# Zero matmuls in every early gap of TensorE, and the first q and k of two head pairs transposed as one planned step

## The chip, the cores and the metric

The kernel runs on one core of a Trainium2 chip. The metric is the device time of one execution in microseconds (us). A profile shows one execution: its span runs from the first to the last instruction, and its own device time stands a little above the span. Engines are written as the profile writes them: PE is TensorE (PEld its weight loads), DVE is VectorE, ACT is ScalarE, POOL is GpSimd and SP is SyncE.

## The reference

Attention over a sliding window of 128 positions with 4 sink positions, for 4 batches, 8 heads, 768 positions and a head dimension of 64, followed by a feed-forward part over all 3072 tokens:

```python
scores = scale * np.matmul(q, k.transpose(0, 1, 3, 2))
keep = is_sink | in_window                  # rel in [0, 128), or position < 4
a = softmax(np.where(keep, scores, -1e9))
x = np.matmul(a, v).transpose(0, 2, 1, 3).reshape(B * S, H * D)
a, b = x @ w1, x @ w2                       # 512 -> 1024
out = (a * b @ w3) @ w_out                  # 1024 -> 1024 -> 512
```

## The kernel before

The whole kernel is a list of steps (class `Op`, L126) that a planner puts in order while the program is built. Each step names its engine, a planned duration, the steps that it depends on, the buffers that it takes and frees, and a priority. The loop at L843 simulates five engines: it takes whatever step can start first, calls the step's function, which writes its instructions to the engine's queue, and books the planned time. The chip then runs each engine's queue in exactly that order, held only by semaphores. So a planned time that changes a little early can reorder steps much later, and a planned time has no power over the chip beyond the order.

Work on TensorE falls into these groups. Batch 0's q and k are transposed (L441) from two layouts in `early` (`early_72` is k and `early_71` is q), copied from PSUM to `qkT` (the copy helper, L143), and multiplied to scores (L597). ScalarE takes the exponential (L615), VectorE multiplies by a mask (L621), TensorE multiplies by v (L673), and VectorE normalises (L683, L688) into `xs`, which is transposed again (L709). The product w3 · w_out is computed once ("the fold"): w3 is transposed in pieces (L351 for the first three row blocks, by column block j; L382 for the other five row blocks) and multiplied by w_out (L359 and L389). The feed-forward part is L753 (x · w1 and x · w2), L768 (their product, on VectorE) and L783 (times the fold), and the result is stored by SP (L800). For batches 2 and 3, q and k are transposed by DMA on SP's queue (L487), and `xs` by L729.

The start is this. ScalarE and SP issue four fast loads of the first two head pairs of k and q (L215; here called k0, q0 for the pair r = 0, and k1, q1 for r = 1), with planned landings of 3.75, 4.05, 5.2 and 5.5 us (L887). k0 and k1 are cast by VectorE and q0 and q1 by ScalarE (L235). All other loads are issued by POOL (L160), one after another in the fixed order of `LOADS` (L243), and at most eight of them are in flight at a time. POOL also builds `ident`, `pick` and `tri` between its loads.

The transposes of a head pair are six matmuls for k and six for q, into one PSUM bank. If (c, r) is in `APART` (L173), the planner has two steps, `a` for k and `a2` for q (L451, L452); otherwise one step that depends on both casts (L454). Their results are copied by two steps, `tk` (k's half) and then `tq` (q's half), each on ScalarE or VectorE, whichever the planner finds free (L457, L458).

Before TensorE starts a step, the planner looks at the gap since its last one (L854). If the gap is over 0.12 us and the plan stands before 45 us, it puts in matmuls of a tile of zeros (L862) into a free PSUM bank, as many as fit the gap less 0.05 us, at most 24 at a time. A matmul over 128 columns is planned at 0.056 us, and at twice that while the plan stands before `WARM` = 5.8 us (L805, L855). These zero matmuls are ordinary instructions: once in the queue they run whether or not real work is waiting behind them.

Of the kernel before, what the change touches and what calls it, by code (L numbers as in the profile page):

```python
# [21 lines left out]
def kernel(  # L22
# [22 lines left out]
    P = 128  # L45
# [92 lines left out]
    PE, ACT, DVE, POOL, SP = "pe", "act", "dve", "pool", "sp"  # L138
# [6 lines left out]
    def cols(n, k=1):  # L145
        return k * (n / 2400.0 + 0.0025)
# [23 lines left out]
    DEEP = 2  # L170
    FUSED = (1, 2, 3)
    KINDS = (0, 2, 2, 2)
    APART = ((0, 0), (0, 1))  # L173
    QK_BY_DMA = ((2, 0), (2, 1), (3, 0), (3, 1))
    X_BY_DMA = ((2, 0), (2, 1), (3, 0), (3, 1))

# [102 lines left out]
    for key in LOADS.split():  # L279
        n = [int(x) for x in key[2 if key[:2] == "wo" else 3 if key[:3] == "w3j" else 1:].split("-") if x.isdigit()]  # L280
# [52 lines left out]
    acc_keys, n = [], 0  # L333
# [85 lines left out]
    for b in range(B):  # L419
# [10 lines left out]
        if b == 0:  # L430
            for c in range(NC):
                for r in range(NP):
# [16 lines left out]
                    pr = base + 1 + r * 0.1  # L449
                    if (c, r) in APART:  # L450
                        a = Op(PE, cols(P, 3) + 0.12, lambda f=tps: f((0,)), [got["k", b, c, r], op_ident], pr, takes=["mm"])  # L451
# [352 lines left out]
    free = {PE: 1.0, ACT: 0.8, DVE: 0.9, POOL: 0.9, SP: 0.8}  # L804
    WARM = 5.8  # L805
# [9 lines left out]
    def unsure(at):  # L815
        return 0.0 if at < 40.0 else 0.5 if at < 56.0 else 2.5
# [11 lines left out]
    def best(e):  # L828
        pick_ = None
        for o in ready[e]:  # L830
            w = wants(o, e) if e != POOL or o is in_order[0] else None
            if w is None:
                continue
            at = max(w, free[e])
            wait = at - free[e]
            key = (0.0 if wait < 0.05 else wait, o.prio, o.serial)
            if pick_ is None or key < pick_[0]:
                pick_ = (key, at, o)
        return None if pick_ is None else (pick_[1], pick_[2])

    with tc.manual_schedule():
        left, lanes = len(ops), []
        while left:  # L843
            moves = []
            for e in free:
                got_ = best(e)
                if got_:
                    moves.append((got_[0], e, got_[1]))
            start, e, o = min(moves, key=lambda x: (x[0], x[1]))
            if e == POOL and hasattr(o, "dma"):  # L850
                if len(lanes) >= 8 and lanes[-8] > start:
                    free[POOL] = lanes[-8]
                    continue
            if e == PE and start < 45.0 and start - free[PE] > 0.12:  # L854
                one = cols(P) * (2 if free[PE] < WARM else 1)  # L855
                n = min(24, int((start - free[PE] - 0.05) / one))
                bank = next((rings[x].slots[i] for x in ("mm", "sc", "av") for i, f in enumerate(rings[x].free)
                             if f is not None and f <= free[PE]), None)
                if bank is not None and n > 0:
                    view = bank[:, 0, 0:P] if len(bank.shape) > 2 else bank[:, 0:P]  # L860
                    for i in range(n):
                        nc.tensor.matmul(view, zeros[:], zeros[:], start=True, stop=True)  # L862
                    free[PE] += n * one
                    continue
            o.slot = {}
            for i, n in enumerate(o.takes):
                f, s = rings[n].soonest()
                rings[n].free[s] = None
                key = (n, i) if o.takes.count(n) > 1 else n
                o.slot[key] = rings[n].slots[s]  # L870
                o.slot["#", key] = s
            turn_of[0] = o.ran = e
            o.fn()
            us = o.us_on[e] * (2 if e == PE and start < WARM else 1)
            free[e] = start + us
            o.done = start + us + o.lat
            if hasattr(o, "turn"):
                dma["at"] = max(dma["at"], start + 0.6) + o.turn
                o.done = max(start + 2.2, dma["at"] + 0.9, dma["sp"] + o.pitch)
                if o in op_vst:  # L880
                    o.done = max(o.done, 11.0)
                else:
                    dma["sp"] = o.done
                    if start < 120.0:
                        o.done += LATE
            if o in st:
                o.done = (3.75, 4.05, 5.2, 5.5)[st.index(o)]  # L887
            if hasattr(o, "dma") and e == POOL:
                dma["at"] = max(dma["at"], start + us + 0.1) + o.dma * 1.02
                while dma["fetch"] and dma["at"] > dma["fetch"][0][0]:  # L890
                    dma["at"] += dma["fetch"].pop(0)[1]
                lanes.append(dma["at"] + LAND)
                o.done = lanes[-1] + unsure(dma["at"])
            for h, n in o.frees:
                h = h[0] if isinstance(h, list) else h
                key = n
                ring = n[0] if isinstance(n, tuple) else n
                rings[ring].free[h.slot["#", key]] = o.done
            for e_ in o.us_on:
                ready[e_].remove(o)  # L900
            if e == POOL:
                in_order.pop(0)
            for u in o.users:
                u.missing -= 1
                if not u.missing:
                    for e_ in u.us_on:
                        ready[e_].append(u)
            left -= 1
# [35 lines left out]
```

## Time and profile before

| what | value |
|---|---|
| runs | 199.4, 200.13, 199.81, 199.07 us; median 199.6 us |
| the profiled execution | 199.4 us, its span 197.7 us |
| TensorE matmuls busy | 191.2 us, 97% of the span |
| VectorE busy | 115.3 us, 58% |
| ScalarE busy | 98.3 us, 50% |
| POOL busy | 73.2 us, 37% |
| zero matmuls (L862) | 79, the first at 1.3 us, the last at 21.3 us |
| transposes of batch 0's q and k (L441) | 96, from 4.6 to 37.0 us |

How to read it: the chain of waits follows the work that ended last back to the start, so each piece on it held the next. A timeline line gives the start, the time to the end of the last instruction in the group, the engine, the line of code, the tiles, the count, and in brackets how long the engine was idle before and who released it. A matmul's time in the trace holds its latency, so the spacing of a group is its time less that of one matmul, divided by the count less one. The 1.7 us between span and time is the same start and end around any execution.

### The profile page before, as it was taken

What the parts mean: (1) busy time and instruction counts of PE and PEld (TensorE: products, weight loads), DVE (VectorE), ACT (ScalarE), POOL (GpSimd) and SP (SyncE); (2) the same over time, 40 slices, a digit from 0 to 9 for tenths busy, and PEclk for the clock granted to TensorE, in tenths of its full rate; (3) what the DMA queues carried; (4) which work ended last, traced back from release to release, by engine and by line L of the source; (5) the groups of instructions that cost most, each with busy time, mean ns of one, the idle gap of its engine ahead of it and who ended that gap; (6) DMA issues with size and microseconds to landing.
All of it is one profiled execution on the core that took longest, in us unless ns stands there. A gap on an engine that the chain in (4) does not pass through costs nothing.

```text
span 197.7 us, 4514 instructions
## 1 busy us (share of the span) xinstructions
PE 191.2 (97%) x1815; PEld 116.8 (59%) x1815; DVE 115.3 (58%) x262; ACT 98.3 (50%) x158; POOL 73.2 (37%) x96
## 2 busy tenths in 40 slices
PE   7989999999999999999999999999999999999993
PEld 6665655546665665567566555655665555555442
DVE  3886523668579756887877763446887543424200
ACT  3785432765466248537547623335477424243233
POOL 7997454787997385656740000000000000000000
PEclk9999999999999999999999999999999999999999
DMA  6999999999999999999999626645503434010133
GB/s 169 175 177 190 202 202 195 182 175 162 153 143 180 148 149 141 210 158 155 155 129 173 86 84 169 149 83 109 133 2 84 107 121 121 0 53 0 56 127 138
DMA packets 98181, 26.42 MB, mean 134 GB/s; under 512 B 86896, under 2 KB 94576, under 8 KB 98160
## 3 DMA queue, kind: packets, MB, share of 16 engines
q0 software_dynamic: 73584, 14.29, 91.6%
q1 hardware_dynamic: 23888, 11.38, 26.9%
q10 hardware_dynamic: 688, 0.46, 0.7%
q8 instruction: 14, 0.23, 0.5%
q14 instruction: 7, 0.06, 0.1%
HBM read 29.39 MB, written 6.29 MB: 181 GB/s over the span
## 4 chain that ended last, share of the span: by engine, by line
PE 87%; DMA 5%; POOL 4%; ACT 1%; DVE 1%; issue 0%
PE mm L753 42%; PE mm L783 21%; PE av L673 7%; PE sc L597 5%; DMA big<-in_moe_w_dram 5%; PE mm L389 5%; POOL big L160 3%; PE mm L862 2%; PE mm L470 1%; ACT qkT L143 1%; PE mm L709 1%; PE mm L382 1%; PE mm L535 1%; PE mm L441 1%; DVE qkT L143 1%
## 5 line engine op out<-in xcount | busy, mean ns | idle before, releaser
L753 PE MATMUL mm<-xT,w_sb 128*128 128x384 bf16 x512 | 89.5, 326 | 0.0
L753 PEld LDWEIGHTS <-w_sb 128*128 128x128 bf16 x512 | 48.1, 98 | 32.1 <-issue 1.4
L768 DVE TENSOR_TENSOR ab<-a_sb,mm 128x384 bf16<-128x384 f32 x64 | 35.4, 553 | 31.4 <-PE mm L753 29.8
L615 ACT ACTIVATE ex<-sc 128x1024 bf16<-128x1024 f32 (+2 forms) x49 | 44.0, 938 | 7.9 <-PE sc L597 6.6
L783 PE MATMUL mm<-w3o,ab 128*128 128x512 bf16 (+2 forms) x208 | 45.9, 363 | 0.0
L143 ACT COPY a_sb<-mm 128x384 f32<-128x384 f32 x51 | 24.4, 479 | 41.1 <-PE mm L753 22.0
L621 DVE TENSOR_TENSOR am<-ex,maskt 128x1024 bf16<-128x1024 bf16 (+2 forms) x49 | 29.8, 624 | 0.9 <-ACT ex L615 0.8
L783 PEld LDWEIGHTS <-ab 128*128 128x128 bf16 x208 | 18.6, 98 | 17.7 <-issue 0.6
L160 POOL DMA_DIRECT2D vN<-in_v_dram x24 | 21.2, 884 | 11.2 <-DMA near<-in_q_dram 3.2
L143 ACT COPY o_sb<-mm 128x512 f32<-128x512 f32 (+2 forms) x21 | 11.5, 546 | 24.2 <-PE mm L783 24.1
L673 PEld LDWEIGHTS <-am 128*128 128x128 bf16 x352 | 17.1, 97 | 3.5 <-DVE am L621 0.2
L673 PE MATMUL av<-vN,am 128*128 128x65 bf16 x352 | 19.0, 194 | 0.0
L688 DVE TENSOR_TENSOR xs<-av,rec 128x384 bf16<-128x384 f32 x32 | 17.7, 555 | 0.6
L597 PE MATMUL sc<-qkT 64*128 64x128 bf16 (+1 forms) x248 | 14.7, 241 | 0.2 <-ACT ex L615 0.2
L683 DVE RECIPROCAL rec<-av 128x6 f32<-128x6 f32 x32 | 6.2, 194 | 14.1 <-PE av L673 14.0
L160 POOL DMA_DIRECT2D big<-in_q_dram x12 | 10.6, 886 | 6.3 <-DMA vN<-in_v_dram 3.0
L673 PE MATMUL av<-vsb,es 128*128 128x130 bf16 x64 | 12.9, 220 | 0.0
L160 POOL DMA_DIRECT2D big<-in_k_dram x12 | 10.5, 880 | 3.2 <-DMA vN<-in_v_dram 1.7
L597 PEld LDWEIGHTS <-qkT 64*128 64x128 bf16 x248 | 8.1, 94 | 5.6 <-issue 4.0
L143 DVE COPY qkT<-mm 128x384 bf16<-128x384 bf16 (+1 forms) x13 | 6.8, 554 | 5.8 <-PE mm L470 3.1
L389 PE MATMUL mm<-big,w3t 128*128 128x512 bf16 x40 | 9.5, 380 | 0.1
L143 DVE COPY w3t<-mm 128x1024 bf16<-128x1024 bf16 (+1 forms) x8 | 4.5, 564 | 6.8 <-PE mm L382 6.0
(63 smaller groups left out, 142.5 us busy)
## 6 DMA issues: line engine op xcount, KB each, us to landing
out_dram<-o_sb SPq DMA_DIRECT2D x23, 256.0 KB
vN<-in_v_dram POOLq DMA_DIRECT2D x24, 128.0 KB, 9.7
w_sb<-in_moe_w_dram POOLq DMA_DIRECT2D x8, 256.0 KB, 10.3
big<-in_k_dram POOLq DMA_DIRECT2D x12, 128.0 KB, 10.0
big<-in_q_dram POOLq DMA_DIRECT2D x12, 128.0 KB, 10.6
big<-in_moe_w_dram POOLq DMA_DIRECT2D x5, 256.0 KB, 10.8
big<-in_moe_w_out_dram POOLq DMA_DIRECT2D x3, 256.0 KB, 6.3
near<-in_q_dram POOLq DMA_DIRECT2D x6, 128.0 KB, 8.1
```

Source lines behind the costliest of these rows:

```text
L143: (nc.scalar.copy if turn_of[0] == ACT else nc.vector.tensor_copy)(out, in_)
L160: op = Op(eng, us, lambda: (nc.gpsimd if eng == POOL else nc.sync).dma_start(out=out, in_=in_), deps)
L389: nc.tensor.matmul(x[2].slot["mm"][:], x[1].slot["w3t"][:, j, :], wo_sb[:, j, :], start=(j == 0), stop=(j == KFF - 1))
L597: nc.tensor.matmul(sc[:, e, c * P:(c + n) * P], T[hp, r, 0, kb * P:(kb + 1) * P], T[hp, r, 1, qb * P:(qb + n) * P], start=True, stop=True)
L615: nc.scalar.activation(y[1].slot["ex"][:, :, 0:w], y[0].slot[key][:, :, 0:w], ACTF.Exp, scale=scale)
L621: nc.vector.tensor_mul(y[2].slot["am"][:, :, 0:w], y[1].slot["ex"][:, :, 0:w], maskt[:, :, m0:m0 + w].to_broadcast([P, 2, w]))
L673: nc.tensor.matmul(o, lhs, rhs, start=(i == 0), stop=(i == len(todo) - 1), skip_group_check=True)
L683: nc.vector.reciprocal(x[1].slot["rec"][:], av_of(x[0].slot["av"])[:, :, :, D:VW])
L688: nc.vector.tensor_mul(xs_first[c].slot["xs"][:, :, r * P:(r + 1) * P].rearrange("p k (e d) -> p k e d", d=D), av_of(x[0].slot["av"])[:, : ...
L753: nc.tensor.matmul(pg[:, 0:TOK], w_sb[:, kk, dt * P:(dt + 1) * P], holder[0].slot["xT"][:, kk, :], start=(kk == 0), stop=(kk == NP - 1))
L768: nc.vector.tensor_mul(abh[0].slot["ab"][:, dt, :], y[1].slot["a"][:], y[2].slot["mm"][:, 0:TOK])
L783: nc.tensor.matmul(x[0].slot["mm"][:, 0:n1 - n0], abh[0].slot["ab"][:, kk, mi * P:(mi + 1) * P], w3o[:, kk, n0:n1], start=(kk == 0), stop= ...
```

## The change

```diff
-    APART = ((0, 0), (0, 1))
+    APART = ()
...
-            if e == PE and start < 45.0 and start - free[PE] > 0.12:
-                one = cols(P) * (2 if free[PE] < WARM else 1)
-                n = min(24, int((start - free[PE] - 0.05) / one))
+            cold = free[PE] < 8.5
+            if e == PE and start < 45.0 and start - free[PE] > (0.04 if cold else 0.12):
+                one = cols(P) * (2 if cold else 1)
+                n = min(24, int((start - free[PE]) / one) + 1 if cold else int((start - free[PE] - 0.05) / one))
```

The planner now fills every TensorE gap over 0.04 us up to 8.5 us of its plan, counts each zero matmul there at the doubled length, and rounds the number up instead of down, so that the planned fill runs past the gap's end. From 8.5 us on the old rule holds. The planned lengths of real steps still double only before 5.8 us. The first two head pairs are each planned as one step for q and k.

In the built program this makes the following differences, and no others. The nine groups of zero matmuls have 34, 5, 9, 2, 7, 4, 2, 7 and 9 members, where they had 30, 2, 17, 2, 8, 3, 2, 6 and 9; the sum is 79 in both. On TensorE one block moves: the first six L709 transposes stand one fold step (three L359 matmuls) earlier. The first pair's copies swap engines: `tk` goes to VectorE and `tq` to ScalarE, where ScalarE had `tk` and VectorE `tq`. On ScalarE the cast of q1 now stands ahead of the first pair's copy instead of behind it. The second pair's `tq` moves from ScalarE to VectorE, between the two steps that build the masks (L258 and L254). On VectorE one mask multiplication (L621) and one w3t copy swap places. On SP, two of batch 3's DMA transposes (L487) move ahead of one output store each. POOL's order is unchanged. In both programs the first k transpose waits for k's cast alone, and the first q transpose for q's cast: the semaphores do not follow the planner's joint step.

## The prediction

> **What bounds the kernel now.** I read the page's slices first. TensorE is full from the second slice on, so I asked next where its order is last held by something that is not TensorE. The chain of waits, cut to the first 60 us, says it:
>
> ```profile
> 5.54 0.49 ACT qkT L143
> 6.05 0.57 DVE qkT L143
> 6.62 0.31 POOL tri L286
> 6.93 0.84 POOL vN L160
> 7.76 6.85 POOL big L160 x10
> 14.61 9.35 DMA big<-in_moe_w_dram
> 23.96 0.05 issue
> 24.01 0.62 PE mm L382 x8
> 24.63 3.45 PE mm L389 x16
> ```
>
> The columns are start, duration and what. At 24.01 us TensorE starts the second L382 block, released by a load of w3 that POOL issued at 14.61 and that landed at 23.96. Before that the chain runs over POOL, which is busy almost without a break from 1.31 to 16.67 us. (The step from DVE to POOL at 6.62 is inferred: POOL's own load before `tri` ran from 5.68 to 6.61, so POOL was not waiting.) The windows by stage, with time, PE busy, PEld busy and so on, then show what follows:
>
> ```profile
> 0.00:24.00 24.00, 21.25 (x267) 15.08 (x267) 15.32 (x57) 13.98 (x25) 18.75 (x33) 1.00 1.31 182
> 24.00:40.00 16.00, 15.51 (x148) 8.80 (x148) 7.14 (x13) 7.49 (x14) 9.70 (x12) 1.00 1.54 193
> 40.00:80.00 40.00, 40.00 (x410) 25.15 (x409) 28.30 (x62) 22.36 (x33) 30.11 (x36) 1.00 2.27 159
> 80.00:120.00 40.00, 40.00 (x419) 24.79 (x418) 31.15 (x67) 21.10 (x29) 14.68 (x17) 1.00 1.61 141
> ```
>
> From 24 us to the last stage TensorE has half a microsecond of idle time. So the end is the moment at which it passes 24 us, plus a body of matmuls that this change leaves in the same order. What matters is whether TensorE reaches that point late. Its timeline just ahead of it:
>
> ```profile
> 20.57 0.50 PE L351 MATMUL mm<-ident,big 128*128 128x128 bf16 x6
> 20.90 0.67 PE L862 MATMUL sc<-zeros 128*128 128x128 bf16 x9
> 21.52 0.49 PE L709 MATMUL mm<-ident,xs 128*128 128x128 bf16 x6
> ...
> 22.95 0.59 PE L359 MATMUL sc<-big,w3t 128*128 128x512 bf16 x2
> 23.38 0.38 PE L359 MATMUL mm<-big,w3t 128*128 128x512 bf16 x1
> 24.01 0.62 PE L382 MATMUL mm<-ident,big 128*128 128x128 bf16 x8 [0.25 <-DMA big<-in_moe_w_dram]
> ```
>
> The L359 matmuls start 0.215 apart (22.95, and 23.38 two later), so the next could have started at 23.59. It started at 24.01: **0.42 us of slack** (0.25 by the idle count, which leaves out the last matmul's latency). A delay up to this size at the front costs nothing, and a gain at the front brings nothing, because the load lands when it lands.
>
> **The change part by part.** The front in the trace of before:
>
> ```profile
> 4.65 0.85 PE L441 MATMUL mm<-ident,early 128*64 128x128 bf16 x12
> 5.32 0.53 DVE L235 CAST early<-o_sb 128x384 bf16<-128x384 f32 x1
> 5.43 0.39 PE L862 MATMUL mm<-zeros 128*128 128x128 bf16 x2
> 5.54 0.48 ACT L143 COPY qkT<-mm 128x384 bf16<-128x384 bf16 x1 [0.69 <-PE mm L441]
> 5.91 0.51 ACT L235 CAST early<-a_sb 128x384 bf16<-128x384 f32 x1
> 6.05 0.56 DVE L143 COPY qkT<-mm 128x384 bf16<-128x384 bf16 x1 [0.20 <-ACT qkT L143]
> ```
>
> *Zeros, first group.* 30 took 3.38 us from 1.33, a spacing of 0.106. Thirty-four end their issue at 1.33 + 34 x 0.1067 = 4.96. The first transposes go from 4.65 to 4.97: +0.32, since 0.12 of the four added (0.43) fills a real gap. They are twelve in six pairs (the two heads of a pair overlap), 0.107 a pair, so the results are there at 5.82 instead of 5.50. That they are "one step" adds no wait of its own: each half keeps its own semaphore.
>
> *Zeros, second group.* Five at 0.107 run from 5.61 to 6.15. k1's cast ends at 5.85 as before, so k1's transposes start at 6.15, not 5.90: +0.25. q1's cast now comes ahead of ScalarE's copy. When q1 lands, the trace does not show. It had landed by 5.91, and ScalarE can start it at 4.84 at the earliest. Either end gives a cast done by 6.42; the transposes need it at about 6.31. I take a landing near 5.4, as k1's cast started at 5.32 and the two loads are of one size. Then k1 and q1 run through by 6.70; before they ended at 6.84. Gain 0.14; at the late end of the landing, zero.
>
> *First pair's copies.* `tk` on VectorE 5.84 to 6.40 (0.56), then `tq` on ScalarE 6.42 to 6.90 (0.48). The pair ended at 6.61; it ends 0.29 later. Behind them on ScalarE is `tk` of the second pair, and then the exponentials. The scores start at 6.96 instead of 6.77.
>
> *Second pair's `tq` to VectorE.* ScalarE loses a copy worth 0.37 (two of them took 0.86, one 0.48), so the first exponential can start at about 7.3 (its scores are done then) instead of 7.63. VectorE gains one of 0.56. There the masks wait for POOL's `tri` until 6.96 in both programs, so the copy stands in a busy row: masks and memset ended at 8.32 and now end at about 8.86. Queued behind are the mask multiplications (first at 8.49 before, released by the exponential): +0.37. Behind those are the next `qkT` copies (9.35 before) and through them ScalarE's copy at 9.94, which already waited 0.24 for VectorE. So from 10 us on **both engines run about 0.37 late**.
>
> *Where that lag goes.* Three places absorb it: TensorE waits at 13.67 for a piece of w3 (idle 0.37 there); ScalarE has been idle 0.53 before its w3t copy at 14.71, so it can finish its exponentials at 14.56 instead of 14.19; and VectorE has been idle 0.51 at 12.59. The zeros ahead of the fold (15.24) wait for that w3t copy. Seven of them instead of six, at 0.056, put the fold at 15.63 instead of 15.57. TensorE then runs through to 23.65, still ahead of the landing at 23.96. Left: **0.0 us**. If all three covers failed the cost would be 0.37 + 0.06 - 0.42, that is 0.0 again; with the 0.56 copy and the 0.32 of the first group added in full it is 0.88 + 0.06 - 0.42 = 0.5. These are the two ends.
>
> *Moved L709 block.* It now stands at about 16.93. It needs `xs`, ready at 16.61 (VectorE's L688 at 16.06 for 0.55): 0.3 to spare. Below nothing it cannot go, since its time is only moved.
>
> *SP.* A batch-3 transpose (about 1.2) goes ahead of the store at 121.54, and another ahead of the store at 137.65, so each store leaves 1.2 later. Their `o_sb` buffers come round after three stores (from the list of SP's queue, at about 151 and 158), so nothing waits. Cost nothing.
>
> *Clock.* The granted clock in the rows is 1.00 throughout, so it does not show the start; the spacing does. Pairs 0.107 apart at 4.65 become (0.44 - 0.31) / 2 = 0.06 apart from 5.90 on. [...] By the trace it came at about 5.95, through gaps at 5.3 to 5.4 and 5.7 to 5.9, so there was nothing to rescue in this execution. [...]
>
> **Sum.** 199.4 (span 197.7 and 1.7 around it) plus 0.0. The profiled execution lies 0.2 under the median of the runs shown (199.6). I take 199.5. A measurement of this kernel can tell about 0.5%, or 1.0 us, from no change.
>
> **The rivals.**
> 1. *Late at the fold (slower).* VectorE's added copy, with the first pair's delay, passes down the chain and is not absorbed at 13.67 or 14.7. For it: both engines are 75 to 98% busy in each 2 us from 8 to 14. Against it: the idle times named. It decides from 0.42 us of lag at 15.57. Price 0.5, or 0.94 where the w3 load lands early and gives no slack: 199.9 to 200.4, say 200.1.
> [...]
> 3. *It does not do what it says.* The q and k semaphores are still apart and the hardware's gaps differ from the plan's, so the time is that of before: 199.6.
> 4. *The w3 load itself moves.* VectorE's added copy meets POOL's descriptor work; the profile's `tri` copies on VectorE stretch from 0.19 to 0.61 while POOL issues loads. If POOL gave way by a whole copy, the landing would be 0.56 later: 200.0. Against it: ScalarE's moved copy is one in 15 us of POOL time.
>
> **How the numbers follow.** Absorbed, with rival 3: 0.64, 199.5, own range 199.0 to 200.0. Rival 1: 0.16, a good half of it under +1.0. Rival 2: 0.12. Rival 4: 0.08. Measured medians also move by some 0.3. Faster by over 0.5%: 0.11; slower by over 0.5%: 0.14, mostly rival 1 with no slack; the rest, 0.75, within. Range 198.8 to 200.5.
>
> **What would show it.** First transposes at about 4.97 and second at 6.15; first exponential near 7.3; first mask multiplication near 8.86; fold start at 15.6; L382 at 24.0 still released by the load, with less idle before it. If the fold starts after 16.0, rival 1 holds. If the load lands away from 23.9, rival 4 or its opposite does. The forecast fails if the body after 24 us changes length at all.

## The result, and the profile after

The changed kernel takes 199.59 us (median of 35 runs, 199.1 to 201.89) and the kernel before 199.58 us (56 runs): a ratio of 1.0006, with a 95% interval from 0.9994 to 1.0018. Nothing that can be measured has changed; the interval reaches from 0.1 us faster to 0.4 us slower. Ratios leave out the executions that took over 1.5% more than the fastest of the same kernel, among them three of 281 to 837 us. The profiled execution took 199.28 us, its span 197.6 us (before: 199.4 and 197.7).

First four pieces of the chain of waits of the changed kernel (start, duration, what):

```profile
6.96 0.82 DVE maskt L258 x3
9.04 0.89 DVE am L621 x2
15.30 0.55 PE mm L863 x7
22.09 0.58 PE mm L382 x8
```

POOL's ten loads of w3 and the long wait behind them are gone from it; POOL's first loads, up to `tri` at 6.62, are still there. What comes last now runs through VectorE's masks and the mask multiplications at 9.04, and reaches the fold through the zero matmuls at 15.30 (L863 is the L862 of before). TensorE's timeline shows the same:

```profile
15.30 0.55 PE L863 MATMUL mm<-zeros 128*128 128x128 bf16 x7
15.69 0.59 PE L359 MATMUL sc<-big,w3t 128*128 128x512 bf16 x2
...
21.59 0.49 PE L709 MATMUL mm<-ident,xs 128*128 128x128 bf16 x6
22.07 0.61 PE L382 MATMUL mm<-ident,big 128*128 128x128 bf16 x8
...
23.59 0.38 PE L359 MATMUL mm<-big,w3t 128*128 128x512 bf16 x1
23.80 0.61 PE L382 MATMUL mm<-ident,big 128*128 128x128 bf16 x8
```

The second L382 block starts at 23.80, straight behind its forerunner (23.59 plus 0.21), where before it waited until 24.01. This time TensorE came last, not the load. At the first block there is a gap of 0.14 us (21.59 plus six times 0.056 is 21.93, and it started at 22.07). This gap is not a wait for a load. VectorE's copy of w3t just ahead of it started at 21.17 before, released by TensorE; now it waits for ScalarE's copy:

```profile
21.17 0.36 DVE L143 COPY w3t<-mm 128x384 bf16<-128x384 bf16 x1 [0.26 <-PE mm L351]
```

```profile
21.66 0.36 DVE L143 COPY w3t<-mm 128x384 bf16<-128x384 bf16 x1 [0.68 <-ACT w3t L143]
```

(The first line is of before.) The L382 block starts 0.05 us after the end of that copy, at 22.02, and in all nine traces of kernels with the changed kernel's order it starts 0.46 to 0.48 us after the L709 block (0.33 before). So this wait belongs to the change, and neither the list of differences nor the prediction has it. The body, from the second L382 block to the end of the span, is 173.8 us (173.7 before), and TensorE is as busy in it:

```profile
24.00:40.00 16.00, 15.52 (x152) 8.78 (x151) 7.54 (x14) 7.69 (x14) 9.16 (x12) 1.00 1.54 193
80.00:120.00 40.00, 40.00 (x419) 24.75 (x417) 31.10 (x66) 21.10 (x29) 15.15 (x18) 1.00 1.65 146
```

And the front, as a timeline:

```profile
5.07 0.85 PE L441 MATMUL mm<-ident,early 128*64 128x128 bf16 x12
5.47 0.51 ACT L235 CAST early<-a_sb 128x384 bf16<-128x384 f32 x1 [0.66 <-DMA a_sb<-in_q_dram]
5.86 0.47 PE L863 MATMUL mm<-zeros 128*128 128x128 bf16 x5
6.26 0.53 PE L441 MATMUL mm<-ident,early 128*64 128x128 bf16 x12
7.09 0.45 PE L597 MATMUL sc<-qkT 64*128 64x256 bf16 x6 [0.30 <-ACT qkT L143]
7.45 0.56 DVE L143 COPY qkT<-mm 128x384 bf16<-128x384 bf16 x1
9.04 0.89 DVE L621 TENSOR_TENSOR am<-ex,maskt 128x768 bf16<-128x768 bf16 x2
10.44 0.94 ACT L143 COPY qkT<-mm 128x384 bf16<-128x384 bf16 x2 [0.92 <-DVE qkT L143]
```

The first transposes came at 5.07 (4.65 before), ScalarE's second-half copies at 10.44 (9.94 before), with 0.92 us of idle time ahead of them (0.24 before), because VectorE's copy that they wait for came late. So the front is half a microsecond late at 10 us, and at the fold, 15.69, it is 0.12 us late.

### The profile page after: what moved, and what is told of

The parts are those of the page before. It is cut to its first block, busy times and chain, and to the rows that moved or that the text cites. A ratio compares the mean times of both kernels' runs of the same rounds, so it can differ in the third digit from the quotient of the medians.

```text
span 197.6 us, 4515 instructions
## 1 busy us (share of the span) xinstructions
PE 191.3 (97%) x1815; PEld 117.4 (59%) x1815; DVE 116.3 (59%) x263; ACT 98.1 (50%) x157; POOL 73.2 (37%) x96
## 4 chain that ended last, share of the span: by engine, by line
PE 90%; DVE 3%; POOL 3%; ACT 2%; issue 1%; POOLq 0%; DVEq 0%
PE mm L753 41%; PE mm L783 21%; PE av L673 7%; PE sc L597 6%; PE mm L389 5%; PE sc L359 2%; PE mm L709 1%; PE mm L470 1%; ACT qkT L143 1%; DVE qkT L143 1%; PE mm L382 1%; POOL vN L160 1%; PE mm L359 1%; PE mm L351 1%; POOL early L160 1%
## 5 line engine op out<-in xcount | busy, mean ns | idle before, releaser
L621 DVE TENSOR_TENSOR am<-ex,maskt 128x1024 bf16<-128x1024 bf16 (+2 forms) x49 | 29.8, 624 | 0.6 <-ACT ex L615 0.4
L143 ACT COPY o_sb<-mm 128x512 f32<-128x512 f32 (+2 forms) x21 | 11.5, 546 | 24.2 <-PE mm L783 24.1
L143 DVE COPY qkT<-mm 128x384 bf16<-128x384 bf16 (+1 forms) x14 | 7.3, 554 | 5.7 <-PE mm L470 3.1
```

Source lines behind the costliest of these rows:

```text
L143: (nc.scalar.copy if turn_of[0] == ACT else nc.vector.tensor_copy)(out, in_)
L621: nc.vector.tensor_mul(y[2].slot["am"][:, :, 0:w], y[1].slot["ex"][:, :, 0:w], maskt[:, :, m0:m0 + w].to_broadcast([P, 2, w]))
```

## Experiments

The theory: what is late at the front is absorbed by waits between 10 us and 24 us. Its rivals: the two parts of the change cancel each other; a late front passes on to the end; the early clock is what counts. In the kernels that only change the zero matmuls, the planner books the old number `n`, so that nothing else moves. `fills` counts the calls that put zeros in (the first group takes two). Ratios are to the kernel before, on the same chip.

### Each part alone

The new fill rule with `APART` as before, and the old fill rule with `APART` empty.

```diff
-    APART = ((0, 0), (0, 1))
+    APART = ()
```

> The new fill rule with the transposes planned apart as before (zero groups 32, 2, 9 at the start; some VectorE steps reorder around 12 to 16 us). If the slack ahead of the w3 load and the waits at 10 to 15 us absorb the front: 199.6, ratio 0.998 to 1.002. If the joint step costs something that the fill repays (the two parts cancel): this one faster by 0.3 us or more, 199.2.

> The joint step with the old fill rule (zero groups 33, 4, 14 at the start; the planner reorders many fold and copy steps up to 40 us, and the fold's last transposes with them). Absorbed: 199.6, ratio 0.998 to 1.002. If the two parts cancel in the changed kernel: slower here by 0.3 us or more, 199.9 and over. Either way VectorE takes over the second pair's q copy and the first mask multiplication comes about 0.4 us later than before (8.9).

Measured: fill alone 199.44 us, ratio 1.0015 (0.9992 to 1.0038); joint step alone 199.68 us, ratio 1.0017 (0.9989 to 1.0044). Neither differs from the kernel before, nor from the changed kernel, so no large gain and loss cancel in it. But in both profiled executions the granted clock was well below full for a while: 0.55 from 9.0 to 11.5 us with fill alone, and 0.50 from 15 to 18 us with the joint step alone. With fill alone (200.19 us) this follows a gap; below it are the windows (time, PE busy, PEld, DVE, ACT, POOL, then the granted clock, the DMA share and GB/s):

```profile
7.53 0.36 PE L441 MATMUL mm<-ident,early 128*64 128x128 bf16 x6 [1.01 <-ACT qkT L143]
```

```profile
6.00:9.00 3.00, 1.99 (x26) 1.36 (x27) 1.79 (x9) 1.96 (x4) 2.99 (x5) 0.81 1.74 177
9.00:11.50 2.50, 2.50 (x36) 1.82 (x34) 1.50 (x4) 1.51 (x4) 2.50 (x5) 0.55 2.04 163
```

The gap is ahead of q1's transposes. Their weight load waited until 7.15 for ScalarE's cast of q1, which itself waited 0.75 us for its load and began at 6.59 (5.47 in the changed kernel's profile). The transposes then waited until 7.53 for the copy that ScalarE ran behind the cast. So most of the gap comes from a late load, and the last 0.38 us from the order of ScalarE's steps. In the joint kernel's execution (202.0 us; first mask multiplication at 8.62, so only 0.13 us late) the gap is a wait for a load too. TensorE's timeline and its windows:

```profile
14.20 0.34 PE L351 MATMUL mm<-ident,big 128*128 128x128 bf16 x3 [1.58 <-DMA big<-in_moe_w_dram]
...
17.05 1.45 PE L862 MATMUL mm<-zeros 128*128 128x128 bf16 x13
```

```profile
14.00:15.00 1.00, 0.80 (x16) 0.71 (x17) 0.00 (x0) 0.42 (x2) 0.55 (x1) 0.92 1.27 184
15.00:18.00 3.00, 3.00 (x29) 2.28 (x28) 1.66 (x6) 1.95 (x4) 2.78 (x5) 0.50 1.26 198
18.00:19.00 1.00, 1.00 (x18) 0.88 (x18) 0.61 (x3) 0.00 (x0) 0.55 (x1) 0.87 1.27 212
```

After a wait of 1.58 us for a load of w3, the clock was at half from about 14.84 to 18.26 ((1 - 0.92) x 2 = 0.16 and (1 - 0.87) x 2 = 0.26 in the outer windows), and thirteen zero matmuls took 1.45 us. Four of the 14 runs of this kernel had a mean clock of 0.992 or less and took 201.9 to 202.7 us; of the kernel before on this chip, 1 of 44 runs had such a clock. Why this kernel's clock falls more often stays open. This asked for a test of its own, below.

### A late front

```diff
-                    for i in range(n):
+                    for i in range(n + 10 * (len(fills) == 1)):
```

> The changed kernel with ten more zero matmuls in the first group (44 for 34), nothing else moved: TensorE's first transposes start 1.07 us later, at 6.1. If the waits behind absorb a late front: most of it is gone by the fold (start 15.7 to 16.0 against 15.69), and the time is 199.6 to 199.9. If the front passes on to the end: 200.3 to 200.7.

Measured: 199.73 us, ratio 1.0014 (0.9993 to 1.0035). Its timeline:

```profile
5.80 0.53 PE L441 MATMUL mm<-ident,early 128*64 128x128 bf16 x12
...
15.86 0.38 PE L359 MATMUL sc<-big,w3t 128*128 128x512 bf16 x1
...
23.98 0.61 PE L382 MATMUL mm<-ident,big 128*128 128x128 bf16 x8
```

The transposes came at 5.80, 0.73 us after the changed kernel's (the 44 zeros took 4.54 us, where a spacing of 0.106 throughout gives 4.87: the last of them ran closer together, hence not 1.07). The fold started 0.17 us later, and 24 us was passed 0.18 us later. Three quarters of the delay were gone by the fold in this execution, and the median is 0.2 us over the changed kernel's, with some 0.5 us to either side. "A late front passes on" is wrong.

### A delay at the fold

Eight and eighteen more zero matmuls (0.45 and 1.0 us), right ahead of the fold; with eighteen:

```diff
-                    for i in range(n):
+                    for i in range(n + 18 * (len(fills) == 9)):
```

> The changed kernel with eight more zero matmuls (0.45 us) right ahead of the first fold matmul, where nothing behind but the w3 load can absorb them. If the slack of 0.42 us at the second L382 block that the trace of before shows is there in most executions: no more than 0.1 us over the changed kernel, 199.6. If TensorE itself is by now what comes last at 24 us (the changed kernel's trace shows no wait there, and 0.14 us at the first L382 block): 0.3 to 0.45 us more, ratio 1.002.

> The same with eighteen more (1.0 us). Slack of 0.42: 0.6 us more than the changed kernel, 200.2. Slack of 0.14 or none: 0.86 to 1.0 us more, ratio 1.0045 to 1.005. If the front has no bearing on the end at all: 199.6.

Measured: 199.82 us, ratio 1.0016 (0.9999 to 1.0033), and 200.5 us, ratio 1.0046 (1.003 to 1.0063). With eighteen:

```profile
16.91 0.59 PE L359 MATMUL sc<-big,w3t 128*128 128x512 bf16 x2
...
25.02 0.61 PE L382 MATMUL mm<-ident,big 128*128 128x128 bf16 x8
```

In this execution the fold started 1.22 us later than in the changed kernel and 24 us was passed 1.22 us later (0.22 of this was there before the zeros, which started at 15.52): nothing was absorbed. By the ratios, the eighteen cost (1.0046 - 1.0006) x 199.6 = 0.8 us over the changed kernel, and the eight 0.2. That leaves about 0.2 us of slack between the fold and the end, with some 0.4 us to either side by the intervals, so none at all is as likely. The trace with eight shows none either: 0.45 us late at the fold (16.14) and 0.46 at 24 us (24.26).

### The zeros taken out

The last two groups (fold and second L709 block) in the changed kernel, twice, and in the kernel before, with the changed kernel itself beside the second:

```diff
-                    for i in range(n):
+                    for i in range(n * (len(fills) < 9)):
```

> The changed kernel without its last two groups of zero matmuls (7 ahead of the fold, 9 ahead of the second L709 block: 0.89 us of TensorE time). If the w3 load sets 24 us: 0 to 0.3 us gained, 199.3 to 199.6. If TensorE sets it: 0.6 to 0.9 us gained, 198.7 to 199.0.

> The changed kernel once more, beside the next two on one chip. As before: ratio 0.999 to 1.002, granted clock dipping in about one run of twenty.

> The changed kernel without its last two groups of zero matmuls, a second time, since the first interval just reached 1. If the gain is real: ratio 0.997 to 0.9995, about 0.4 us under the changed kernel. If it was scatter: 1.000 and the changed kernel's own value.

> The kernel before without the same two groups (6 ahead of the fold and 9 ahead of the second L709 block, 0.84 us of TensorE time). If these groups cost the same whatever the front does: 0.3 to 0.5 us under the kernel before, ratio 0.9975 to 0.9985. If the w3 load or another wait takes their place: 1.000.

Measured: 199.12 us, ratio 0.9989 (0.9973 to 1.0004); then, on one chip, the changed kernel 199.56, ratio 1.0011 (0.9993 to 1.0028), without the groups 199.34, ratio 1.0001 (0.9984 to 1.0018), and the kernel before without them 199.25, ratio 0.9999 (0.9984 to 1.0014). The gain of the first run did not come back clear of scatter, and nothing beats the kernel before. The 0.89 us of zeros is replaced by other waits (changed kernel without the groups, second run):

```profile
15.59 0.39 PE L359 MATMUL sc<-big,w3t 128*128 128x512 bf16 x1 [0.36 <-DMA big<-in_moe_w_out_dram]
...
21.51 0.49 PE L709 MATMUL mm<-ident,xs 128*128 128x128 bf16 x6 [0.45 <-ACT w3t L143]
...
23.72 0.61 PE L382 MATMUL mm<-ident,big 128*128 128x128 bf16 x8
```

Without zeros the fold waits for a load of w_out, and L709 waits for ScalarE's w3t copy. TensorE passes 24 us at 23.72, against 23.80 with the zeros. These zeros stand in real gaps. The kernel before without them shows one thing more:

```profile
21.79 0.61 PE L382 MATMUL mm<-ident,big 128*128 128x128 bf16 x8
23.53 0.61 PE L382 MATMUL mm<-ident,big 128*128 128x128 bf16 x8
```

TensorE does not wait for w3 ahead of the second L382 block, although it arrives half a microsecond ahead of the 24.01 of before. From block to block it takes 1.74 us, which is the time of the matmuls between the starts (8 x 0.056 + 6 x 0.215). In the trace of before it is 2.16. Of the twelve traces that show both blocks (the joint kernel orders these steps differently) that one alone has a wait for the load there, though in five of the others TensorE gets there before 24.01.

The profiled execution of the changed kernel's second run also shows where the scatter at full clock can come from:

```profile
13.59 0.34 PE L351 MATMUL mm<-ident,big 128*128 128x128 bf16 x3 [1.10 <-DMA big<-in_moe_w_dram]
...
24.69 0.50 PE L382 MATMUL mm<-ident,big 128*128 128x128 bf16 x6
```

A load of w3 landed late, TensorE waited 1.10 us for it at 13.59 (in the first profile that block ran at 12.71), and 24 us was passed 0.89 us later; the span was 198.3 us instead of 197.6.

### The early and the middle zeros

Without the first three groups (48 zeros), and without the third to the eighth (31 zeros):

```diff
-                    for i in range(n):
+                    for i in range(0 if cold else n):
```

```diff
-                    for i in range(n):
+                    for i in range(n * (not 4 <= len(fills) <= 9)):
```

> The changed kernel without its first three groups of zero matmuls (48 of 79), all else in the same order. The clock then comes later: transposes and scores up to at least 8.5 us at the half-clock spacing of 0.107. If the slack hides the early clock: 199.6 to 200.0, with the transposes of the first pair 0.4 us earlier (4.65). If an early clock is what the zeros buy: slower by 0.5 us or more, 200.1 to 200.8.

> The changed kernel with its first two groups kept and the next six left out (31 zero matmuls from 7.4 to 15.7 us). If the clock, once released, holds through such gaps: 199.3 to 199.7, all runs at a mean clock of 0.995 or over. If the zeros keep it up: in a quarter or more of the runs the granted clock dips (mean 0.993 or less) and these take 200.5 to 203 us; the median rises by 0.3 us or more.

Measured: without the early ones 200.4 us, ratio 1.0054 (1.0038 to 1.0071), so they are worth 1 us. Its timeline (L864 is the zeros' line in this kernel):

```profile
4.43 0.93 PE L441 MATMUL mm<-ident,early 128*64 128x128 bf16 x12 [4.43 <-POOL pick L267]
...
11.85 0.93 PE L864 MATMUL mm<-zeros 128*128 128x128 bf16 x7
...
12.94 0.40 PE L864 MATMUL mm<-zeros 128*128 128x128 bf16 x4
```

The first transposes are 0.64 us earlier than in the changed kernel (4.65 was expected), but zeros at 11.85 are still 0.107 apart and only those at 12.94 are 0.06 apart, as those at 5.86 are in the changed kernel. So full speed came some 7 us later, and the fold started at 16.46, 0.77 us late; 24 us was passed 0.77 us late too (24.57).

Without the middle ones the median is 199.7 us, ratio 1.0007 (0.9993 to 1.0021): the same time as the changed kernel. In 16 of 22 runs the mean clock was 0.993 or less (199.27 to 202.22 us, median 199.80), and the median of the other six was 199.21 us. (Of the kernel before on this chip it was 3 of 60 runs.) So these zeros do keep up the clock. The expectation that such runs take at least 200.5 us and lift the median by 0.3 us was too high. It may be that the fall of the clock costs what the absent zeros save, but that is not shown: the six runs are few, and they may be those whose loads came early. In the profiled execution (200.5 us), by windows:

```profile
11.50:12.50 1.00, 0.28 (x2) 0.09 (x1) 0.98 (x3) 1.00 (x3) 1.00 (x2) 1.00 1.50 169
12.50:13.50 1.00, 0.14 (x3) 0.14 (x4) 0.00 (x0) 0.74 (x2) 0.83 (x2) 1.00 1.33 181
13.50:14.50 1.00, 1.00 (x21) 0.79 (x20) 0.75 (x3) 0.12 (x1) 0.79 (x2) 0.94 1.22 179
14.50:15.50 1.00, 1.00 (x11) 0.58 (x9) 1.00 (x4) 0.69 (x1) 1.00 (x2) 0.50 1.19 184
15.50:16.50 1.00, 1.00 (x15) 0.89 (x14) 0.52 (x3) 0.68 (x2) 1.00 (x3) 0.50 1.19 192
16.50:17.50 1.00, 1.00 (x3) 0.30 (x2) 0.85 (x3) 0.68 (x2) 0.62 (x2) 0.50 1.19 174
17.50:18.50 1.00, 1.00 (x8) 0.54 (x7) 1.00 (x7) 0.48 (x1) 0.47 (x1) 0.85 1.19 177
```

TensorE is idle for most of two microseconds (waits of 0.62 and 1.15 us, the second for a load of w3), and a granted clock of 0.50 follows from 14.5 us on, when it is busy again.

## Why the prediction was right, point by point

The forecast was 199.5 us with the time inside 0.5%. That held. The steps from 10 us to the fold held in mechanism and nearly in size. The last cover, 0.42 us of slack at 24 us, did not hold, and that the time came out right in spite of it is partly luck: there was little for it to cover, 0.06 us by the forecast and about 0.2 us by the traces, which is too little to measure here.

*First transposes.* Forecast 4.97, measured 5.07. I had taken the 0.12 us from the last zero to the first transpose for a gap that zeros would fill. It is a step that stays: without the early zeros the transposes started at 4.43, so they were not waiting for data, and four more zeros moved them by 0.42, nearly their full 0.43. The second pair, 6.15 against 6.26, is partly luck: its zeros started at 5.86 instead of 5.61, but ran about 0.06 us apart instead of 0.107: five of them took 0.47 us, so full speed came just then. The 0.1 us went on into the scores (6.96 against 7.09) and the first exponential (7.3 against 7.47). Both starts also change with the clock: in the second profile of the changed kernel full speed came sooner (the twelve first transposes took 0.58 us instead of 0.85), and they stood at 4.82.

*q1's landing.* Estimated near 5.4, measured: ScalarE's cast waited for it until 5.47 (in the execution with fill alone, until 6.59).

*VectorE's added copy.* First mask multiplication 8.86 forecast, 9.04 measured (8.49 before); lag at ScalarE's copies 0.37 forecast, 0.50 measured (10.44 against 9.94). The size was low for a reason of its own, since the masks began at 6.96 as forecast: they ended at 8.93 instead of 8.86, and the first multiplication started 0.11 us after that instead of at once.

*Where the lag goes.* Forecast: absorbed by 15.6, with the fold at 15.63. Measured 15.69, and by two of the three places named. Before:

```profile
12.97 0.34 PE L597 MATMUL sc<-qkT 64*128 64x256 bf16 x4
13.68 0.51 PE L351 MATMUL mm<-ident,big 128*128 128x128 bf16 x6 [0.37 <-DMA big<-in_moe_w_dram]
14.71 0.48 ACT L143 COPY w3t<-mm 128x384 bf16<-128x384 bf16 x1 [0.53 <-PE mm L351]
```

After:

```profile
13.46 0.34 PE L597 MATMUL sc<-qkT 64*128 64x256 bf16 x4
13.73 0.51 PE L351 MATMUL mm<-ident,big 128*128 128x128 bf16 x6
14.77 0.48 ACT L143 COPY w3t<-mm 128x384 bf16<-128x384 bf16 x1
```

TensorE is 0.49 us late at the scores and 0.05 late at the L351 block behind them: its wait for w3 took up the rest. ScalarE is 0.44 late at its exponentials (12.46 against 12.02) and 0.06 late at the w3t copy, whose 0.53 of idle time is gone. The fold's 0.12 is this 0.06 and the seventh zero. The run with ten more zeros shows the same on a larger scale: 0.73 us at the transposes, 0.17 us at the L351 block (13.90) and at the fold.

*The slack at 24 us.* This step was right for the execution it was read from and wrong as a property of the kernel. I had TensorE arriving at 23.65 and waiting until 24.01. It arrived at 23.80, 0.21 us later than the 23.59 of before, and did not wait, since the load was there by then (it landed at 23.96 before). Of the 0.21, 0.12 is the fold's and 0.14 the wait for VectorE's w3t copy, less 0.05 between them. Of the twelve traces only the one of before has the wait for the load, so the sum had no slack to take off, and a cost of about 0.2 us is what the traces suggest. The ratios of the two sets, 1.0006 and 1.0011, are 0.1 and 0.2 us, and neither can be told from nothing.

*The moved L709 block and SP's order.* L709 ran at 16.98 (forecast 16.93) without a wait, and the body from 24 us on kept its length. SP's two swaps cost nothing that any window shows.

*Rivals.* Late at the fold did not happen at more than 0.12 us; its price was roughly right, as the run with 18 zeros shows. The moved w3 load did not happen as I had it: the load came earlier in this execution. That the change doesn't do what it says is half true: the transposes of q and k still followed their own casts, and gaps that the plan does not know stayed open on TensorE (0.30 us ahead of the scores at 7.09, and 0.43 ahead of the first L351 block at 10.40).

*The clock.* I gave 0.12 to a gain where full speed would otherwise come late. That it first comes at a different time in different executions is so: 34 zeros took 3.81 us in the changed kernel's profile and 3.40 us in the one without the middle zeros, whose start is the same. But no run shows that denser zeros bring it forward, nor a gain from it: the changed kernel's ratios are 1.0006 and 1.0011. Removing the early zeros costs 1 us (ratio 1.0054), so the zeros of before already bought the early full speed, and denser ones added nothing that can be measured. What can still cost time is a later fall of the clock, behind waits that the plan does not know (201.9 to 202.7 us in the four such runs of the joint kernel). Runs at a mean clock of 0.993 or less were 5 of 161 for the kernel before in the three sets of experiments, and 3 of 57 for the changed kernel (201.4 to 202.0 us): too few to tell apart, and no sign of fewer.

What stays open: the scatter of 199.0 to 200.5 us at full clock. One late load is shown to go with 0.7 us of span; that late loads make the whole scatter is only argued, and the body after 24 us is not the same in every execution either (174.3 us in the one without the early zeros). Open too is why the clock falls in one execution and not in another.

## What to carry to other kernels

In this kernel the early filler matmuls were worth 1 us, by bringing full speed early (ratio 1.0054 without them), and the last two groups, where TensorE waited anyway (0.36 and 0.45 us), nothing that could be measured (1.0001 without them, 1.0011 with them on the same chip). So ask for each group of fillers which real wait it covers, by taking that group out alone. A slack that one trace shows is one draw (0.42 us here, behind a wait that eleven other traces lack). Before a sum rests on it, put a known delay ahead of it and see how much comes through.

## What the runs showed of the hardware

The granted clock in the rows reads 1.00 at the start, while the changed kernel's first zeros are 0.106 us apart and those at 7.47 are 0.058 apart, so when full speed first comes has to be read from spacings. A later fall does show. The granted clock was 0.50 from about 14.38 to 17.80 without the middle zeros ((1 - 0.94) x 2 = 0.12, three full windows, (1 - 0.85) x 2 = 0.30), that is 3.42 us, and 3.42 us again in the joint kernel (14.84 to 18.26). It fell behind waits of 1.58 us in one piece in the joint kernel, and of 0.62 and 1.15 us with little between them without the middle zeros. Size alone does not decide it: the second profiled execution of the changed kernel waited 1.10 us at 13.59, and its mean granted clock was 1.00, while with fill alone the clock fell to 0.55 behind a gap of 1.01 us. No run here isolates what does.
